# First gate and up units over two feature chunks and both columns, with 256-wide matmuls; 39 spins on a constant tile; gelu table behind column 1's copy

## Chip, cores, metric

One core of one Trainium2 chip. The metric is the device time of one execution in microseconds; lower is better. Before: 178.17 us (median of 6 runs, 177.86 to 178.23).

## The reference, cut to what matters

```
x  = A_x                                    # 1 x 2048 x 512, bf16
xn = layernorm(x)                           # over the last axis
h  = gelu(xn @ w_gate) * (xn @ w_up)        # 512 -> 1792
return x + irfft2(rfft2(xn) * W) + h @ w_down
```

The change touches the start only: normalising the first rows and the first gate and up matmuls.

## The kernel before

PE is the tensor engine, DVE the vector engine, ACT the scalar engine, POOL GpSimd, and SP issues the transfers. PSUM holds the tiles named `..._ps` in the kernel, into which its matmuls write. "Spins" are matmuls whose result is never used: they keep PE busy until the input is there, so that its granted clock rises from half to full speed ("released") early. (In the profile before, 128-wide matmuls start every 107 ns up to 6.49 us and every 55 ns from 6.78 on.) Four more of them, the "fillers" (`spin_on`), bridge the time between the first transposes and the first gate matmul.

The 2048 rows lie as 16 "columns" of 128 rows. Columns 0 and 1 go first: statistics on DVE, square root on ACT, normalisation on DVE, transposes on PE, copies from PSUM on ACT and DVE. Gate and up then run in units: `c0, n` are the first column and the number of columns, `f0, m` the first feature chunk of 128 and their number. The moving operand is `n` x 128 wide. The first four units (k < 4) split the contraction (four chunks `e`) in halves, so that the first half can start before all has landed.

```python
    spin = pc.tile([P, P], BF16, name="spin")
    ...
    nc.vector.memset(spin[:], 0.0)
    nc.vector.memset(eps_t[:], EPS)
    ...
    sp_ps = ps.tile([P, D], F32, name="sp_ps", tag="S", bufs=4)
    for k in range(37):
        pin(nc.tensor.matmul(sp_ps[:, :P], lhsT=spin[:], rhs=spin[:], start=True, stop=True))
    ...
        table = add("ACT", 1.3, lambda: A.activation(out=warm[:], in_=eps_t[:], func=AF.Gelu_apprx_tanh), [o["root", 1]], key=-1500, lat=1.3)
    ...
        o["copyt1"] = add("ACT", 0.4, lambda: f_Tc(1, 2, 2, A.copy), [o["t", 1], table], key=-1400)
    ...
        def mm_part(name, tag, W_, e0):
            if e0 == 0:
                b[name] = ps.tile([P, m, w], F32, name=name, tag=tag, bufs=2)
            for e in (e0, e0 + 1):
                for f in range(m):
                    T_.matmul(b[name][:, f], lhsT=W_[:, e, (f0 + f) * P:(f0 + f + 1) * P], rhs=rhs[:, e, :],
                              start=(e + f == 0), stop=(e == NE - 1), skip_group_check=True)
    ...
    todo = [(0, 1, 0, 4), (0, 1, 4, 4), (1, 1, 0, 4), (1, 1, 4, 4)]
    todo += [(2, 2, f, 2) for f in range(0, 8, 2)]
    todo += [(0, 4, f) for f in range(8, NFC)]
    todo += [(4 * sb, 4, f) for sb in range(1, NSB) for f in range(NFC)]
```

A planner in the program simulates the engines with assumed durations (`add(engine, duration, function, dependencies, key=...)`) and so fixes each engine's order when the program is built.

## Time and profile before

| | before |
|---|---|
| median time | 178.17 us |
| span of the profiled execution | 176.6 us |
| PE busy | 171.9 us (97%) |
| chain that ended last | PE 97% |
| first spin, first gate matmul, first up matmul | 1.05, 5.96, 10.13 us |
| end of the last matmul | 173.80 us |

Read it from the end: the last matmul's end plus some 2.8 us for the last addition and store is the span. PE runs without gaps from 5.96 on, so a date at which PE reaches a given piece carries over to the end unchanged, unless PE waits later.

### The profile page before, as it was taken

The numbers are of one execution on the slowest core, as the hardware profiler recorded it, in microseconds if no ns is written. First come the engines' busy times: TensorE is split into PE (matmuls) and PEld (weight loads), VectorE is DVE, ScalarE is ACT, GpSimd is POOL, SyncE is SP. The second block draws the span as 40 slices with busy tenths as digits, with TensorE's granted clock in tenths as the row PEclk, the third lists the DMA queues.
The fourth block names the chain that finished last, engine by engine and source line by source line (L and its number), as shares of the span: only waits on it lengthen the run. The fifth ranks groups of instructions, "written<-read, shape, count | busy, mean of one in ns | idle before, by whom it ended". The sixth has DMA issues, their size and how long they took to land.

```text
span 176.6 us, 3179 instructions
## 1 busy us (share of the span) xinstructions
PE 171.9 (97%) x1158; PEld 97.6 (55%) x1175; DVE 115.7 (66%) x253; ACT 96.8 (55%) x174; POOL 17.4 (10%) x38
## 2 busy tenths in 40 slices
PE   7999999999999999999999999999999999999993
PEld 7999844555545554555555445454444445444463
DVE  3459999987433699979899999643616325345333
ACT  4662299799646988898899955362112111211200
POOL 1020250504771000000000000000000000000000
PEclk9999999999999999999999999999999999999999
DMA  5999986432726902201211520200122222221212
GB/s 137 333 397 380 324 202 106 91 65 60 231 67 198 335 8 57 59 22 43 59 27 38 146 50 14 59 4 0 59 89 89 84 70 72 76 89 60 63 59 59
DMA packets 20847, 19.35 MB, mean 110 GB/s; under 512 B 8480, under 2 KB 17952, under 8 KB 20832
## 3 DMA queue, kind: packets, MB, share of 16 engines
q1 hardware_dynamic: 20416, 17.84, 34.3%
q0 software_dynamic: 416, 1.32, 2.5%
q8 instruction: 9, 0.15, 0.4%
q14 instruction: 6, 0.05, 0.1%
HBM read 13.38 MB, written 2.10 MB: 88 GB/s over the span
## 4 chain that ended last, share of the span: by engine, by line
PE 97%; issue 1%; DVE 0%
PE y_ps L837 27%; PE g_ps L492 25%; PE u_ps L492 25%; PE sp_ps L320 2%; PE g_ps L500 2%; PE yp L788 2%; PE bp L597 2%; PE u_ps L500 2%; PE gp L758 2%; PE dp L655 2%; PE y_ps L841 2%; PE ep L664 2%; PE tp L351 1%; PE sp_ps L324 0%; DVE y_sb L844 0%
## 5 line engine op out<-in xcount | busy, mean ns | idle before, releaser
L492 PE MATMUL u_ps<-xnT,Wu_sb 128*128 128x512 bf16 (+1 forms) x219 | 52.7, 363 | 0.2
L492 PE MATMUL g_ps<-xnT,Wg_sb 128*128 128x512 bf16 (+1 forms) x217 | 52.4, 363 | 0.4
L837 PE MATMUL y_ps<-Wd_sb,hT 128*128 128x512 bf16 (+2 forms) x247 | 50.5, 355 | 0.2
L510 DVE TENSOR_TENSOR hT<-u_ps,ge 128x512 bf16<-128x512 f32 x56 | 38.1, 688 | 17.7 <-PE u_ps L492 15.2
L505 ACT ACTIVATE ge<-g_ps 128x512 bf16<-128x512 f32 x56 | 33.4, 602 | 21.7 <-PE g_ps L492 19.0
L837 PEld LDWEIGHTS <-hT 128*128 128x128 bf16 x252 | 23.2, 98 | 22.5
L492 PEld LDWEIGHTS <-Wu_sb 128*128 128x128 bf16 x224 | 21.5, 98 | 20.8
L492 PEld LDWEIGHTS <-Wg_sb 128*128 128x128 bf16 x224 | 21.4, 98 | 20.2
L794 ACT CAST yf<-yp 128x512 bf16<-128x512 f32 x16 | 9.3, 586 | 40.5 <-PE yp L788 40.5
L844 DVE TENSOR_TENSOR y_sb<-y_ps,y_sb 128x512 bf16<-128x512 f32 (+2 forms) x18 | 11.1, 631 | 30.0 <-PE y_ps L841 30.0
L669 ACT CAST E<-ep 64x512 bf16<-64x512 f32 x32 | 18.5, 579 | 1.4 <-PE ep L664 1.0
L339 DVE BATCH_NORM_STATS2 stats<-x_t 128x6 f32<-128x512 bf16 x16 | 10.5, 674 | 3.2 <-DMA x_t<-in_A_x_dram 3.2
L454 ACT ACTIVATE xn<-x_t,nb,rstd 128x512 bf16<-128x512 bf16 x12 | 9.5, 814 | 1.0 <-POOL nb L370 1.0
L567 ACT CAST ds<-dp 128x512 bf16<-128x512 f32 x16 | 9.2, 598 | 0.8 <-PE dp L655 0.8
L567 ACT CAST Gs<-gp 128x512 bf16<-128x512 f32 x16 | 8.7, 592 | 0.6 <-PE gp L758 0.5
L567 ACT CAST Bs<-bp 128x512 bf16<-128x512 f32 x16 | 8.5, 611 | 0.5 <-PE u_ps L492 0.5
L800 DVE TENSOR_TENSOR lv<-yf 128x512 bf16<-128x512 bf16 x16 | 6.1, 421 | 1.5 <-ACT yf L794 0.6
L788 PEld LDWEIGHTS <-Gs 128*128 128x128 bf16 x64 | 4.8, 98 | 3.5
L807 DVE TENSOR_TENSOR yt<-lv 128x512 bf16<-128x512 bf16 x16 | 6.1, 422 | 0.3
L788 PE MATMUL yp<-CT,Gs 128*128 128x128 bf16 x64 | 6.0, 219 | 0.1
L841 PE MATMUL y_ps<-yt,RI_t 128*128 128x512 bf16 (+2 forms) x18 | 6.1, 355 | 0.0
L664 PE MATMUL ep<-ds,CT 128*128 128x512 bf16 x16 | 5.7, 379 | 0.0
(68 smaller groups left out, 134.1 us busy)
## 6 DMA issues: line engine op xcount, KB each, us to landing
F<-F SPq DMA_DIRECT2D x32, 64.0 KB, 2.0
y_sb<-in_A_x_dram SPq DMA_DIRECT2D x16, 128.0 KB, 2.1
out_dram<-y_sb SPq DMA_DIRECT2D x15, 128.0 KB, 1.7
x_t<-in_A_x_dram SPq DMA_DIRECT2D x7, 256.0 KB, 8.9
Wd_sb<-in_B_w_down_dram SPq DMA_DIRECT2D x1, 1792.0 KB, 8.5
Wg_sb<-in_B_w_gate_dram SPq DMA_DIRECT2D x2, 512.0 KB, 4.7
Wu_sb<-in_B_w_up_dram SPq DMA_DIRECT2D x2, 512.0 KB, 7.0
Wg_sb<-in_B_w_gate_dram SPq DMA_DIRECT2D x1, 768.0 KB, 10.4
```

What stands on the lines that cost most here:

```text
L339: V.bn_stats(out=st[:], in_=x_t[:, c, :])
L454: xn_op[c] = add("ACT", 0.72, lambda c=c: A.activation(out=xn[:, c, :], in_=x_t[:, c, :], func=AF.Identity, bias=nb[:, c:c + 1], scale=rst ...
L492: T_.matmul(b[name][:, f], lhsT=W_[:, e, (f0 + f) * P:(f0 + f + 1) * P], rhs=rhs[:, e, :], start=(e == 0), stop=(e == NE - 1))
L505: A.activation(out=b["ge"][:], in_=b["g_ps"][:], func=AF.Gelu_apprx_tanh)
L510: V.tensor_tensor(out=hT_of(sb, f0, m, o, w), in0=b["u_ps"][:], in1=b["ge"][:], op=ALU.mult)
L567: A.copy(out=o, in_=i)
L669: A.copy(out=b["E"][64 * h:64 * h + 64, r], in_=b["ep", h][64 * r:64 * r + 64])
L788: T_.matmul(t[:, q], lhsT=late["G"][:, q, c0 + j], rhs=IQ[q], start=(q == 0), stop=(q == 3), skip_group_check=True)
L794: A.copy(out=b["yf"][:, j], in_=b[j][:])
L837: T_.matmul(b[o][:], lhsT=hT_of(sb, f, 1, cl * P, P)[:, 0], rhs=Wd_sb[:, f, o:o + w], start=(f == 0), stop=False)
L841: T_.matmul(b[o][:], lhsT=late["RI"][:, c, :], rhs=late["yt"][:, c, o:o + w], start=False, stop=True)
L844: V.tensor_tensor(out=b["y"][:, o:o + w], in0=b[o][:], in1=b["y"][:, o:o + w], op=ALU.add)
```

## The change

Intent: make the first units cheaper by wider matmuls, start the spins earlier without waiting for DVE's fill, and take column 1's copy out from behind the load of the gelu table. The core of the diff (bookkeeping of dependencies cut):

```diff
-    spin = pc.tile([P, P], BF16, name="spin")
+    spin = nc.const_aps.tensor(1.0, (P, P), BF16)
...
-    nc.vector.memset(spin[:], 0.0)
...
-    for k in range(37):
-        pin(nc.tensor.matmul(sp_ps[:, :P], lhsT=spin[:], rhs=spin[:], start=True, stop=True))
+    for k in range(39):
+        pin(nc.tensor.matmul(sp_ps[:, :P], lhsT=spin, rhs=spin, start=True, stop=True))
...
-        table = add("ACT", 1.3, lambda: A.activation(out=warm[:], in_=eps_t[:], func=AF.Gelu_apprx_tanh), [o["root", 1]], key=-1500, lat=1.3)
...
-        o["copyt1"] = add("ACT", 0.4, lambda: f_Tc(1, 2, 2, A.copy), [o["t", 1], table], key=-1400)
+        o["copyt1"] = add("ACT", 0.4, lambda: f_Tc(1, 2, 2, A.copy), [o["t", 1]], key=-1400)
+        add("ACT", 1.3, lambda: A.activation(out=warm[:], in_=eps_t[:], func=AF.Gelu_apprx_tanh), [o["copyt1"]], key=-1300, lat=1.3)
...
-        def mm_part(name, tag, W_, e0):
+        def mm_part(name, tag, W_, e0, a, z):
...
-                    T_.matmul(b[name][:, f], lhsT=W_[:, e, ...], rhs=rhs[:, e, :],
+                    T_.matmul(b[name][:, f, a:z], lhsT=W_[:, e, ...], rhs=rhs[:, e, a:z],
...
+            args = "g_ps", gt, Wg_sb
+            g = part(*args, 1000, 5.7, 0, 0, P, ...)        # first half of e, column 0
+            g = part(*args, 1000.1, 5.7, 0, P, w, ...)      # first half of e, column 1
+            g = part(*args, 1000.2, 7.8, 2, 0, w, ...)      # second half, both columns, 256 wide
+            args = "u_ps", ut, Wu_sb
+            u = part(*args, 1001, 9.7, 0, 0, w, src)        # up: 256 wide throughout
...
+            u = part(*args, 1001.1, 11.0, 2, 0, w, [u])
...
-    todo = [(0, 1, 0, 4), (0, 1, 4, 4), (1, 1, 0, 4), (1, 1, 4, 4)]
+    todo = [(0, 2, f, 2) for f in range(0, 8, 2)]
```

## The prediction

The sum of the forecast came to -0.12 us, thus 178.04 us: 48 joins of two narrow matmuls at 2.4 ns each (115 ns, from the rates of the profile before), and 0 each for spins and table.

> **What bounds the kernel now.** I read the page's busy table and its chain first, then the chain in order of time, then the timeline of the first 14 us, and the DVE and ACT rows of the same stretch.
>
> ```profile
> span 176.6 us, 3179 instructions
> ...
> PE 171.9 (97%) x1158; PEld 97.6 (55%) x1175; DVE 115.7 (66%) x253; ACT 96.8 (55%) x174; POOL 17.4 (10%) x38
> ...
> PE 97%; issue 1%; DVE 0%
> ```
>
> PE carries the whole chain. A busy PE row alone doesn't prove that PE never waits[...]. So I checked it with the chain in order of time, where each piece has its start, its length and its matmul count:
>
> ```profile
> 1.05 4.12 PE sp_ps L320 x37
> 5.17 0.56 PE tp L351 x4
> 5.74 0.43 PE sp_ps L324 x4
> 6.17 0.78 PE g_ps L500 x8
> 6.94 0.22 PE tp L351 x4
> 7.17 3.13 PE g_ps L500 x56
> 10.29 1.79 PE u_ps L500 x32
> 12.08 0.45 PE tp L351 x8
> 12.53 1.79 PE u_ps L500 x32
> 14.31 1.75 PE g_ps L492 x16
> ```
>
> The reader can take three rates from it: 1.79/32 = 55.9 ns for a 128-wide matmul, 1.75/16 = 109.4 ns for a 256-wide one (the L492 rows of that stretch), and, from a later piece of 14 matmuls in 3.02 us, 215.7 ns for a 512-wide one. The program issues, after the first eight gate matmuls, 418 matmuls or transposes 128 wide, 79 of 256 and 625 of 512 (the program's own instruction list, as a few records are missing in the trace). That is 418 x 0.0559 + 79 x 0.1094 + 625 x 0.2157 = 166.8 us. Those eight end at 6.95, so a PE that never waits would end at 173.8; the chain's last PE piece ends at 173.82. **From 6.95 to the end PE loses less than 0.1 us to waits.** What is left is a store of some 2.8 us behind the last matmul, which the change doesn't touch.
>
> So the time is: the date at which real work starts, the cold rate at the start, and the number and width of matmuls. The start is a latency chain:
>
> ```profile
> 0.36 0.11 POOL L885 MEMSET const-bfloat16-1.0<- 128x1 bf16 x1
> ...
> 0.88 0.11 DVE L263 MEMSET spin<- 128x64 uint32 x1 [0.88 <-PEq L885]
> ...
> 1.05 4.13 PE L320 MATMUL sp_ps<-spin 128*128 128x128 bf16 x37 [1.05 <-DVE minus_half L266]
> ...
> 3.03 0.69 DVE L339 BATCH_NORM_STATS2 stats<-x_t 128x6 f32<-128x512 bf16 x1 [2.02 <-DMA x_t<-in_A_x_dram]
> ...
> 5.46 0.69 ACT L354 COPY xnT<-tp 128x256 bf16<-128x256 bf16 x2
> ...
> 6.17 1.28 ACT L412 ACT_TABLE_LOAD   x1
> ...
> 8.99 2.06 ACT L505 ACTIVATE ge<-g_ps 128x512 bf16<-128x512 f32 x4 [1.07 <-PE g_ps L500]
> ...
> 11.21 0.73 DVE L345 TENSOR_SCALAR xn<-x_t,mv,rstd 128x512 bf16<-128x512 bf16 x2 [1.18 <-POOL rstd L361]
> ```
>
> The input lands at 3.03, and statistics, normalisation, transposes and the ACT copy bring the first gate matmul to 5.96. The spins only fill the time before that, to warm PE's clock. They are not on this chain.
>
> [...] Here the spins start every (4.96 - 1.05)/36 = 109 ns, the gate matmuls from 5.96 to 6.49 still every 107 ns, and the transposes at 6.78 to 7.00 every 55 ns: the release came at about 6.6 to 6.7, although the page's PEclk row shows 9 from the start. [...]
>
> **The change, part by part.**
>
> *Wider matmuls.* Today the first four units are 4 feature chunks by 1 column, all 128 wide: 64 for gate and 64 for up. After, each has 2 chunks by 2 columns: the gate's first halves stay 128 wide (32), its second halves are 16 of 256, and up is 32 of 256. So 96 narrow ones become 48 wide ones: 48 x (2 x 55.9 - 109.4) = 48 x 2.4 = 115 ns[...]. All lie in the stretch where PE never waits: **-0.12 us**.
>
> *Spins.* The constant is filled in the preamble at 0.36 to 0.47, so PE no longer waits for DVE's fills; it can start where the other engines are released, at about 0.80 to 0.85, against 1.05. The 39 spins take 38 x 0.109 to the last start: 0.83 + 4.14 = 4.97, against 4.96 before. So the transposes at 5.03 are met as before: **0**, except through the clock release, below.
>
> *Gelu table behind column 1's copy.* Column 1's second copy runs today at 7.57, after the table load (6.17 to 7.46) and the dummy activation. After, it runs once its transposes end (7.00 + about 0.2), so at about 7.2 to 7.6. It is needed by the first second-half gate group, which PE reaches at 7.00 + 24 x 0.056 = 8.34; before, the column 1 units needed it somewhat later still. So column 1 is ready in time either way. The table then loads from about 7.6 to 8.9 and the dummy ends at about 9.1. The first gelu, today at 8.99, comes at about 9.1, the four of them end at 11.16 instead of 11.05. The fourth up unit needs the bank that the fourth gelu frees, at about 11.2; PE is there at about 10.03 + 3 x 0.4376 = 11.34. Slack is left: **0**.
>
> *Order.* The list of PE instructions is the same up to the first 512-wide units but for the widths. Afterwards the scheduler swaps some spectral groups with their gate or up neighbours; the sum of PE work is the same.
>
> Sum: -0.12 us, thus 178.16 - 0.12 = 178.04.
>
> **Rivals.**
>
> *The clock is released earlier.* If the release follows the start of the spins, it comes 0.2 us earlier, at about 6.45, and PE does the work of 0.2 us in half the time: -0.1 us. [...] For: the dates above. Against: it can't all be kept. Columns 2 and 3 are normalised by DVE from 11.21 to 11.94, a date set by a DMA at 8.53 and POOL. The fifth of the eight transposes follows 5 x 0.056 into a group whose weight loads start at 11.86, so at 12.08; it could start at about 11.99 (other transposes start 0.05 after their DVE row). So everything gained before 12 us is capped at about 0.09, of which the widths already take 0.08 by then; the second up halves add 0.04. **The cap leaves a total of about -0.13 to -0.2 whatever the clock does.** The banks freed by gelu cap it at a similar size.
>
> *A new wait replaces it.* Column 1's first gate group needs DVE's copy (7.09 to 7.38) and PE is there at 7.45; up needs its weights, which PE takes from 10.07 on today; the later swaps could put a spectral matmul ahead of the copy that feeds it. For: margins of 0.05 to 0.15. Against: before, the same copy met PE at the same date without a wait, and the planner left no wait in 167 us. It would make +0.1 to +0.3 us.
>
> *The spins on a broadcast constant run slower or the release comes later.* If they overran 5.03 they would delay the transposes one to one, +0.2 or more. Nothing in this profile speaks for it; I give it little.
>
> **Range and chances.** The sum is -0.12; the first rival pulls by a few hundredths, the second pushes by about as much with less chance. I say 178.0. Three runs of before lie between 177.98 and 178.18, and the profiled one took 178.28, so the noise is as large as the effect; the range is 177.75 to 178.3. 2% is 3.6 us, thirty times the effect; the only part of that size would be a lost clock, which nothing suggests: faster 0.01, same 0.985, slower 0.005.
>
> **What would show it.** In the profile after: spins from about 0.83, and the last transposes of column 0 still at about 5.35; the first gate matmul at 5.9 to 6.0; column 1's ACT copy ahead of the table load; the second gate halves and up at 109 ns each; up starting at about 10.0; the transposes of columns 2 and 3 at 11.75 to 11.85, waiting for DVE if the clock came early; the 256-wide gate group of columns 2 and 3 0.1 to 0.15 us before 14.15; and from there on the same pieces, shifted. The prediction is wrong if that shift is over 0.25, if DVE's second normalisation comes earlier, or if a wait on PE shows up later than 15 us.

## The result, and the profile after

After: 177.93 us (median of 6 runs, 177.78 to 178.14) against 178.17 us (177.86 to 178.23) for the kernel before in the same rounds. The ratio is 0.9991, with a 95% interval of 0.9978 to 1.0004. (A ratio is the mean time of one kernel's fast runs over that of the other's of the same rounds, so it is not quite the ratio of the medians.) By the 2% measure this is "same", and the interval includes no change at all.

The chain that ended last, in order of time, of the changed kernel (start, length, piece, count):

```profile
0.84 4.24 PE sp_ps L319 x39
...
5.63 0.22 PE sp_ps L323 x4
5.88 0.62 PE g_ps L499 x8
6.50 0.22 PE tp L350 x4
6.72 3.09 PE g_ps L499 x40
9.81 1.88 PE u_ps L499 x16
11.69 0.57 PE tp L350 x8
12.26 1.75 PE u_ps L499 x16
14.01 1.75 PE g_ps L491 x16
```

Set against the lines in the prediction: the gate piece of 56 took 3.13 us, its successor of 40 takes 3.09; the second half of up took 1.79, now 1.75. That is the width, as worked out. But the gate group of columns 2 and 3 starts at 14.01 instead of 14.31: 0.30 us earlier, not 0.12. The fillers show where it comes from: four took 0.43 us before (107 ns each) and take 0.22 now (55 ns each). In this execution the clock was already released. The timeline of the same kernel shows what PE then ran into (in brackets the idle time ahead, and what ended it):

```profile
5.87 0.45 PEld L499 LDWEIGHTS <-Wg_sb 128*128 128x128 bf16 x8 [0.20 <-DMA Wg_sb<-in_B_w_gate_dram]
...
6.56 3.25 PE L499 MATMUL g_ps<-xnT,Wg_sb 128*128 128x128 bf16 x40
...
6.76 0.37 ACT L353 COPY xnT<-tp 128x256 bf16<-128x256 bf16 x1 [0.72 <-PE tp L350]
7.15 1.28 ACT L423 ACT_TABLE_LOAD   x1
...
8.55 2.05 ACT L504 ACTIVATE ge<-g_ps 128x512 bf16<-128x512 f32 x4
...
9.77 1.64 PEld L499 LDWEIGHTS <-Wu_sb 128*128 128x128 bf16 x16 [0.24 <-DMA Wu_sb<-in_B_w_up_dram]
...
11.07 0.73 DVE L344 TENSOR_SCALAR xn<-x_t,mv,rstd 128x512 bf16<-128x512 bf16 x2 [1.18 <-POOL rstd L360]
```

Both weights now land after PE is ready for them, and the eight transposes take 0.57 us instead of 0.45, as the fifth waits 0.09 us for DVE's second normalisation. So the early clock release was about half given back to transfers. (An estimate from these dates: a release before 5.9 instead of at 6.73 saves half of 0.83 us, 0.42; of it 0.30 - 0.12 = 0.18 us was kept.) Two questions remained: is the early release a property of the change, and is the 0.12 us of the widths real?

The trace also keeps a record of each change of PE's granted clock. Before: the release is recorded at 6.73 us and the first close spacing of matmuls comes at 6.78, so the two agree. After: 4.86 us. (The page's PEclk row shows 9 from the first slice in both, since the time ahead of the first record is not counted as throttled.) All "release" dates below are such records.

### The profile page after: what moved, and what is told of

Same layout as the page of the kernel before. It is cut to its first block, busy times and chain, and to the rows that moved or that the text cites. A ratio compares the mean times of both kernels' runs of the same rounds, so it can differ in the third digit from the quotient of the medians.

```text
span 176.3 us, 3102 instructions
## 1 busy us (share of the span) xinstructions
PE 172.6 (98%) x1129; PEld 96.4 (55%) x1129; DVE 115.3 (65%) x252; ACT 97.1 (55%) x174; POOL 17.1 (10%) x38
## 4 chain that ended last, share of the span: by engine, by line
PE 98%; DVE 0%; issue 0%
PE y_ps L835 27%; PE g_ps L491 25%; PE u_ps L491 25%; PE sp_ps L319 2%; PE g_ps L499 2%; PE u_ps L499 2%; PE yp L786 2%; PE dp L653 2%; PE bp L595 2%; PE gp L756 2%; PE y_ps L839 2%; PE ep L662 2%; PE tp L350 1%; DVE y_sb L842 0%; PE sp_ps L323 0%
## 5 line engine op out<-in xcount | busy, mean ns | idle before, releaser
L491 PE MATMUL g_ps<-xnT,Wg_sb 128*128 128x512 bf16 (+1 forms) x224 | 53.1, 364 | 0.0
L835 PE MATMUL y_ps<-Wd_sb,hT 128*128 128x512 bf16 (+2 forms) x252 | 51.2, 355 | 0.0
L699 DVE TENSOR_TENSOR m<-X,TW 128x1024 bf16<-128x1024 bf16 x8 | 5.5, 688 | 0.2
```

The source lines that it names most:

```text
L835: T_.matmul(b[o][:], lhsT=hT_of(sb, f, 1, cl * P, P)[:, 0], rhs=Wd_sb[:, f, o:o + w], start=(f == 0), stop=False)
```

## The experiments

Twelve runs in four groups; each group shared its runs of the kernel before.

### Both kernels again, and the parts alone

`same_before` and `same_after` are the two kernels unchanged. `spins_only` is the kernel before with only the spins of the change; `wide_only` the one with only the units and widths; `table_only` (of the second group) with only the table's move:

```diff
# spins_only, on the kernel before
-    spin = pc.tile([P, P], BF16, name="spin")
+    spin = nc.const_aps.tensor(1.0, (P, P), BF16)
-    nc.vector.memset(spin[:], 0.0)
-    for k in range(37):
+    for k in range(39):
# wide_only, on the changed kernel: those lines and the table's two lines put back
# table_only, on the kernel before: only the table's two lines as in the change
```

Two theories stand in the expectations: S, that the clock's release follows from what the program issues, and F, that its date changes from execution to execution. Where F's reasons, and ranges of dates worked out from them, had not been shown by a trace, they are cut from the texts here and below.

> The kernel before, unchanged, once more: the null test, ratio 1.000 within 0.1%. Theory F [...]: [...] not again at 6.6 to 6.7[...]. Theory S (the release follows from what the program issues): release again at 6.6 to 6.7[...].

> The changed kernel, unchanged, once more: 177.9, ratio 0.9985 to 0.9995 against before. Theory F: [...] most likely later than the 4.85 of the first profile. Theory S: again at 4.8 to 4.9.

> Only the spins of the change (constant tile, 39). Theory S (the earlier start, or the constant, brings the release to 4.85): release at 4.8 to 4.9 and the time down by 0.15 to 0.25 us, to about 177.95. Theory F: the start is 0.2 us earlier, so the release is 0.2 us earlier on average and 0.1 us at most is gained; the time is 178.1, not to be told from before in 5 rounds.

> Only the units over two columns with 256-wide matmuls; old spins, old place of the table load. Both theories: 0.12 us less, 178.05; up's 16 matmuls before the transposes take 1.75 us instead of 32 in 1.79. The release is drawn as for before: S says 6.6 to 6.7, F says anywhere.

> The kernel before with only the gelu table moved behind column 1's copy. My step: no change of time, ratio 1.000; the copy starts at about 7.1 instead of 7.57, the first gelu at about 9.1. If column 1's copy had held the tensor engine, 0.1 us or more would be gained.

Measured: `same_before` 178.21 us, ratio 1.0003 (0.9986 to 1.0019); `same_after` 178.05, ratio 0.9999 (0.9983 to 1.0014); `spins_only` 178.16, ratio 1.0006 (0.9989 to 1.0024); `wide_only` 178.10, ratio 1.0000 (0.9984 to 1.0016); the kernel before in these rounds 178.05. `table_only` 178.18 against 178.22, ratio 1.0000 (0.9987 to 1.0012). No part, nor the whole, can be told from nothing by time; the 0.9991 of the first six runs was not repeated by the next five.

The dates of one profiled execution each tell more (us; the last column is the difference of the two before it, t3_later is told further down):

| kernel | first spin | clock released | columns 2, 3 normalised from | up starts | last matmul ends | up to end |
|---|---|---|---|---|---|---|
| before | 1.05 | 6.73 | 11.21 | 10.13 | 173.80 | 163.67 |
| same_before | 1.05 | 6.20 | 11.03 | 10.03 | 173.71 | 163.68 |
| table_only | 1.05 | 6.30 | 10.90 | 9.96 | 173.63 | 163.67 |
| spins_only | 0.84 | 4.94 | 11.00 | 9.81 | 173.49 | 163.68 |
| wide_only | 1.05 | 3.98 | 11.30 | 10.01 | 173.72 | 163.71 |
| after | 0.84 | 4.86 | 11.07 | 9.77 | 173.50 | 163.73 |
| same_after | 0.84 | 5.40 | 11.20 | 10.07 | 173.67 | 163.60 |
| t3_later | 0.84 | 3.96 | 10.79 | 9.66 | 173.26 | 163.60 |

Three readings follow.

*The widths are real and of the predicted size.* From up's start to the end, every kernel with narrow up matmuls takes 163.67 to 163.68 us, and the changed one, where no wait falls in, 163.60. The runs told further down agree: `before_x1_act`, with narrow up matmuls, has 163.67, and `one_spin`, `wg_on_act` and `after_x1_act`, with wide ones, have 163.59. Up's 32 joins (two narrow matmuls made one) at 2.4 ns are 0.077 us. Where the total is 163.71 and 163.73, the fifth transpose waited for DVE.

*The release is not tied to the program.* The program before had its release at 6.73 and 6.20 us, the changed one at 4.86 and 5.40, and `wide_only`, with the old spins on zeros, 3.98. Theory S named 6.6 to 6.7 and 4.8 to 4.9 and falls.

*What sets up's start changes from execution to execution.* In the very kernel that is unchanged the weights can be what PE waits for, as in `same_before` (timeline):

```profile
10.03 1.79 PEld L500 LDWEIGHTS <-Wu_sb 128*128 128x128 bf16 x32 [0.20 <-DMA Wu_sb<-in_B_w_up_dram]
```

and in `same_after` they landed 0.3 us later than in the first profile of the same kernel:

```profile
10.06 1.64 PEld L499 LDWEIGHTS <-Wu_sb 128*128 128x128 bf16 x16 [0.37 <-DMA Wu_sb<-in_B_w_up_dram]
```

For `table_only`, the step held: column 1's copy ran at 7.03 instead of 7.57, PE pieces of the same lengths, the same 163.67 behind up's start. The first gelu came at 8.83, earlier than the 9.1 expected; the clock was released 0.4 us earlier in this execution.

The expected ratio of `same_after`, 0.9985 to 0.9995, was not met (0.9999), but its interval doesn't exclude it.

### What the spins are worth: one_spin

```diff
-    for k in range(39):
+    for k in range(1):
     def spin_on():
-        for k in range(4):
+        for k in range(1):
```

> The changed kernel with 1 spin instead of 39 and 1 filler instead of 4; the tensor engine's steady work begins at 5.0 us. Theory F [...]: [...] the time up by half of the cold stretch after 5.9 us, 0.5 to 2.5 us, with a spread of the same size between runs. If the spins were idle filling only, the time would stay within 0.2 us of the changed kernel.

Measured: 179.49 us (178.74 to 179.84), ratio 1.0066 (1.0044 to 1.0088), so some 1.2 us over the kernel before of the same rounds. (The changed kernel did not run in them; the run cuts three of the four fillers as well.) The release came at 10.46 us. The timeline of `one_spin`:

```profile
5.79 1.01 PE L499 MATMUL g_ps<-xnT,Wg_sb 128*128 128x128 bf16 x8
...
7.02 4.91 PE L499 MATMUL g_ps<-xnT,Wg_sb 128*128 128x128 bf16 x40
11.77 1.91 PE L499 MATMUL u_ps<-xnT,Wu_sb 128*128 128x256 bf16 x16
```

The reader sees the piece of 40 take 4.91 us instead of 3.25 in the same view of the changed kernel, and up start 2.0 us later. As expected by F, and the spread of 1.1 us between runs is as large as the effect. Here the spins are no idle filling.

### The dates of many releases: bursts

```diff
+    gate = [pc.tile([P, P], BF16, name=f"gate{i}") for i in range(2)]
+    seen = pc.tile([P, 1], F32, name="seen")
+    for i in range(8):
+        for r in range(3):
+            pin(nc.vector.memset(Wd_sb[:], 0.0))
+        pin(nc.vector.memset(gate[i % 2][:], float(i % 2)))
+        for k in range(66 + i):
+            pin(nc.tensor.matmul(sp_ps[:, :P], lhsT=gate[i % 2][:], rhs=gate[i % 2][:], start=True, stop=True))
+        pin(nc.vector.tensor_copy(out=seen[:], in_=sp_ps[:, :1]))
     for k in range(39):
```

> The changed kernel behind eight bursts of 66 to 73 spins each, with an idle tensor engine of about 11 us ahead of each (three long fills on DVE), on a tile of zeros in bursts 1, 3, 5, 7 and of ones in 2, 4, 6, 8; results stay right and the total time, some 150 us longer, says nothing. Each burst draws its own date of release, 8 in one execution. Theory F: all changes of the clock lie on one grid of 3.413 us; [...] zeros and ones don't differ. Rival Z (zeros count less as activity, which would explain that the seven profiles with the constant were released 3.1 to 5.0 us after the first spin and three of four with zeros at 5.1 to 5.7): in the bursts of zeros the release comes over 1 us later than in those of ones at the same place in the grid.

Measured: the result was right; 317.9 us in one run of unknown state, which says nothing, as announced. All fifteen changes of the clock in the record lie on one grid, multiples of 3413 ns apart: releases at 18.22, 35.28, 52.35, 69.42, 86.48, 103.55, 124.03 and 141.10, throttles between them. From a burst's start to its release it took, in order, 4.72, 3.84, 3.40, 3.04, 2.86, 2.65, 5.96 and 4.16 us. The two that decide are the sixth (ones) and the seventh (zeros), in the timeline of `bursts`:

```profile
100.90 5.38 PE L325 MATMUL sp_ps<-gate 128*128 128x128 bf16 x71 [11.85 <-DVE gate L323]
118.07 7.02 PE L325 MATMUL sp_ps<-gate 128*128 128x128 bf16 x72 [11.79 <-DVE gate L323]
```

One more matmul, but 1.6 us more. The sixth burst starts 2.65 us ahead of a grid point and is released there (it fills 78% of the 3.41 us before it). The seventh starts 2.55 us ahead of one (75%) and isn't; it is released at the next. The fifth, on zeros, was released with 2.86 us (84%). So F's grid held for the fifteen changes of this run, and the dates of the eight bursts sort by where they met it: the four that had 2.65 to 3.40 us ahead of their first grid point were released there, the four that had 0.43 to 2.55 us at the next one. What decides it inside PE is not shown. The clock records of the other profiles agree (that of `before_x1_act` is empty), counted in stretches of 3.41 us back from a recorded change: none that was filled to 75% or less was followed by a release (in `before` 66%, with spins from 1.05 to 3.32), and every throttled one filled to 78% or more was (in `wide_only` 86%, from 1.05 to 3.98). Rival Z falls: bursts of zeros were released with 2.86 and 3.40 us of work, each at the first grid point after its start. (That the share differs between zeros and ones inside 75% to 84% isn't excluded.)

An estimate of what the earlier start is worth, from these dates: say that a start at `s` is released between s + 2.6 (between the 2.55 us that did not suffice and the 2.65 that did) and s + 6.0 (3.41 later; the longest burst took 5.96), with every date between equally likely. That gives 3.7 to 7.1 for the old start and 3.4 to 6.9 for the new; the dates in the table lie inside. A release after 5.9, where gate work begins, costs half of the excess (107 ns for a matmul in place of 55). Its mean is (7.06 - 5.9)^2 / (4 x 3.41) = 0.10 us for the old start, (6.85 - 5.9)^2 / (4 x 3.41) = 0.07 for the new: 0.03 us on average, before what the transfers take back. By this estimate it was luck that the first profile of before drew 6.73 and that of after 4.86.

### What width costs: narrow_all

All later gate and up matmuls are cut to 128 wide.

```diff
-                    T_.matmul(b[name][:, f], lhsT=W_[:, e, (f0 + f) * P:(f0 + f + 1) * P], rhs=rhs[:, e, :],
-                              start=(e == 0), stop=(e == NE - 1))
+                    for q in range(0, w, P):
+                        T_.matmul(b[name][:, f, q:q + P], lhsT=W_[:, e, (f0 + f) * P:(f0 + f + 1) * P],
+                                  rhs=rhs[:, e, q:q + P], start=(e + q == 0), stop=(e == NE - 1), skip_group_check=True)
```

> The changed kernel with all later gate and up matmuls cut into pieces 128 wide (64 of 256 into 128, 384 of 512 into 1536). Theory W (width only costs the fixed part of a matmul, 2.4 ns for a 256 and 7.9 ns for a 512, as the rates of the profile before give): 64 x 2.4 + 384 x 7.9 = 3.2 us more than the changed kernel, 181.1. [...]

Measured: 185.0 us (184.01 to 185.97), ratio 1.038 (1.0344 to 1.0417): some 7 us over the changed kernel, not 3.2. The expectation of the total missed. The chain of `narrow_all` in order of time says why:

```profile
17.64 0.89 PE g_ps L492 x16
...
48.13 0.31 issue
...
48.83 0.35 issue
...
49.40 0.50 issue
...
50.28 1.05 issue
...
53.12 1.71 PE g_ps L492 x16
```

Sixteen narrow matmuls take 0.89 us, 55.8 ns each, in place of 0.86 for four of 512: the rate, and with it some 3.1 of the 3.2 us, is confirmed. The rest is something else: around 48 to 51 us PE stands still with nothing to wait for ("issue", 2.2 us in the chain; by the starts of the matmuls 3.0 us are lost there), and the clock is then throttled for 3.41 us (recorded from 52.38 to 55.79), which costs half of it, 1.7 us. From up's start to the end this profile takes 171.30 us, 7.7 more than 163.60, and 3.1 + 3.0 + 1.7 = 7.8. The profiled run took 185.74 us. The recorded clocks of the four runs support this: 185.74 and 185.97 had a granted clock of 0.991, 184.01 and 184.27 of 1.000, so the throttled stretch is the 1.7 us between the two pairs. What causes the "issue" gaps stays open; the program has 5530 instructions in its profile instead of 3102, and no run separates that.

### Lifting the cap of the transfers: wg_on_act, before_x1_act, after_x1_act

Up's start is capped by landing dates (PE's load of up's first weights stood idle for them 0.24 us in the first profile after, 0.37 in `same_after`), so I tried to issue the early transfers sooner, using ACT's queue beside SP's.

```diff
# wg_on_act, on the changed kernel: first half of the first gate weights
+    pin(load_w(Wg_sb, 0, 1024, nc.scalar, e=slice(0, 2)))
     pin(nc.scalar.activation(out=warm[:], in_=eps_t[:], func=AF.Sqrt, bias=eps_t[:], scale=1.0))
     ...
-        for e in range(0, NE, 2):
+        for e in range(2 if T is Wg_sb else 0, NE, 2):
# before_x1_act and after_x1_act: second column of the input
+    pin(load_x(1, 1, nc.scalar))
     pin(nc.scalar.activation(out=warm[:], in_=eps_t[:], func=AF.Sqrt, bias=eps_t[:], scale=1.0))
     pin(load_x(0, 1))
-    pin(load_x(1, 1))
```

> The changed kernel with the first half of the first gate weights issued from the ACT queue at 0.8 us, ahead of ACT's table load, instead of as third transfer of the SP queue at 1.71. Theory D (what caps the gain are the landing dates of the transfers): everything behind it in the queue lands some 0.3 to 0.5 us earlier, up starts at about 9.55, columns 2 and 3 are normalised from about 10.7, no wait before the transposes, and the end comes 0.2 to 0.3 us earlier than in the changed kernel, about 177.7. Rival: ACT pays for the issue (table load and root later) or the second column of the input lands later behind the weights, the chain to the first gate matmul grows by the same, and nothing is gained or 0.3 us is lost.

> The kernel before with the second column of the input issued from the ACT queue at 0.8 us, ahead of ACT's table load, so that every later transfer of the SP queue is issued 0.43 us earlier. Theory D (landing dates cap the start): up's first weights land at about 9.4 instead of 9.77 to 10.1, but this kernel's tensor engine reaches them at 10.0 to 10.1 only when the clock comes late, so it gains 0 to 0.25 us, depending on the release. Rival: the second column lands behind the first weights as it did when those went first, and the time rises by 1 us.

> The changed kernel with the same move. Theory D: up's first weights at about 9.4, columns 2 and 3 normalised from about 10.7, up starts when the gate's second halves end, 9.55 with an early release, the transposes of columns 2 and 3 no longer wait, and the time is 0.2 to 0.3 us below the changed kernel: 177.7. If the gelu's banks cap it instead (first gelu 8.4 to 9.1), up still starts at about 9.8 and nothing is gained. Rival as for the other: 1 us lost.

Measured: `wg_on_act` 179.80 us (178.98 to 181.04), ratio 1.0097 (1.0059 to 1.0136), in two clusters, near 179.0 and from 180.6 to 181.0. `before_x1_act` 178.71, ratio 1.0057 (1.0024 to 1.009); `after_x1_act` 179.10, ratio 1.0071 (1.0046 to 1.0096). All three lose, by less than 2% but clear of noise; theory D's forecast of a gain was wrong. The rivals were right that time is lost, but not all on how. In `before_x1_act` and `after_x1_act` ACT paid nothing that mattered, and the second column did not land behind the weights, as the rival had it. The first column itself landed later: DVE starts on it at 3.89 and 4.06, against 2.96 to 3.43 in the eight profiles of the table:

```profile
3.89 0.69 DVE L339 BATCH_NORM_STATS2 stats<-x_t 128x6 f32<-128x512 bf16 x1 [2.88 <-DMA x_t<-in_A_x_dram]
```

In `wg_on_act` it was the second column, as its rival said, but the loss was 0.8 to 2.8 us and not 0.3. DVE takes this column's statistics ahead of the first column's normalisation, so the whole chain waited for it:

```profile
5.63 0.69 DVE L339 BATCH_NORM_STATS2 stats<-x_t 128x6 f32<-128x512 bf16 x1 [1.43 <-DMA x_t<-in_A_x_dram]
...
6.83 0.61 PE L351 MATMUL tp<-ident_t,xn 128*128 128x128 bf16 x4 [1.72 <-DVE xn L345]
...
8.25 4.89 PE L500 MATMUL g_ps<-xnT,Wg_sb 128*128 128x128 bf16 x40
```

The 1.72 us that PE then idled had a second price: the piece of 40 takes 4.89 us instead of 3.25. The clock record has a release at 4.94, a throttle at 8.35 and a release at 11.76. Here a released clock was lost again after 3.41 us with 1.72 us of idle time in them. How much idle time is enough doesn't come out of these runs: in `bursts` PE was idle for 1.8 us of the 3.41 us that ended at 21.63, and the clock stayed released. One throttled stretch costs half of 3.41 us, 1.7, and the two clusters lie 1.9 us apart in the mean: the three upper runs, the profiled one (181.04 us) among them, had a granted clock of 0.989 to 0.990 by the record, the three lower ones of 0.998 to 1.000.

That what is issued beside the first column takes bandwidth from it is the author's guess; no run separates this from other effects of the second queue. What the two runs with the second column on ACT's queue show is that nothing was gained, and that the first column landed 0.5 to 1.1 us later.

### Taking away the wait for column 3: t3_later

```diff
             if k == 3:
                 between["t", 2].deps.append(u)
-                between["t", 3].deps.append(u)
             u = part(*args, 1001.1, 11.0, 2, 0, w, [u])
+            if k == 0:
+                between["t", 3].deps.append(u)
```

> The changed kernel with column 3's transposes moved behind the first of up's four second halves. Where the normalisation of column 3 caps the gain (the wait of 0.09 us between the fourth and the fifth transpose), that wait is gone and the later groups start 0.1 us earlier for the same start of up: from up's start to the last matmul's end 163.60 instead of 163.73 us. Nothing that time alone could tell from the changed kernel: 177.9.

Measured: 178.10 us (177.70 to 178.36), ratio 0.9999 (0.9984 to 1.0014). In its profile, the chain in order of time:

```profile
9.79 1.78 PE u_ps L499 x16
11.58 0.22 PE tp L350 x4
11.80 0.44 PE u_ps L499 x4
12.24 0.22 PE tp L350 x4
12.46 1.31 PE u_ps L499 x12
13.77 1.75 PE g_ps L491 x16
```

No wait is left between the transposes, and up to end is 163.60, as expected. But this doesn't test the edit: DVE's second row ended at 11.53 here (10.79 + 0.74), and the fifth transpose in its old place would have come at about 11.64 (11.41 + 4 x 0.056), so it would not have waited either; and `same_after` has 163.60 without the edit. That execution is the shortest seen (span 176.0 us), but it also drew the earliest release of the table and the earliest landings of up's first weights and of columns 2 and 3; over six runs the version can't be told from the others. It beats neither kernel measurably.

## Why the prediction was right, step by step

*PE is the bound and never waits after the start.* Held: behind up's start the time was the same to 0.01 us in every profile of a kernel with narrow up matmuls.

*Widths, -0.12 us.* Held term by term: up's part 0.07 to 0.08 (163.67 against 163.60), the gate's 16 joins 0.04 (3.13 against 3.09), and `narrow_all` gave the same rate over 1600 narrow matmuls. The wholes, 178.17 to 177.93 and 178.05 to 178.05, are compatible with it but don't show it. The stated range of 177.75 to 178.3 holds the time of the kernel before too, so that the median fell into it says little.

*Spins, 0 except through the clock.* Held: the spins started at 0.84 and ended in time, and column 0's second transposes stayed at 5.34. (The prediction's date of 4.96 for the last spin is a misreading: 36 spacings of 0.106 us end at 4.86, and those of the changed kernel at 4.84; nothing hangs on it.) The clock's share is 0.03 us by the estimate above, where the first rival spoke of "-0.1 us". That rival supposed a release that follows the start; in the eight profiles of the table it came anywhere from 2.93 to 5.68 us behind the first spin.

*Gelu table, 0.* Held, by `table_only`.

*The cap, "a total of about -0.13 to -0.2 whatever the clock does".* This step failed. The pair of profiles shows -0.30, and with it two of the prediction's own signs of being wrong came true: a shift over 0.25, and DVE's second normalisation earlier (from 11.07 instead of 11.21). I had taken the date of columns 2 and 3 as fixed by the transfer at 8.53, from one profile. In eight profiles DVE's row starts anywhere from 10.79 to 11.30. (The slack of 0.09 us was read rightly, but the sum has a slip: the fifth transpose's weights load four spacings of 0.056 after 11.86, not five, which gives the 12.08 that is written.) The wait itself was seen twice, 0.09 us ahead of the fifth transpose in the first profile after and in `wide_only`; but the date that sets it moves by more than the effect. And the stricter cap in most executions was the one I had only listed among new waits: the landing of up's first weights. In five of the eight profiles their load stood idle 0.14 to 0.37 us for it, in a rerun of the kernel before too, which cost the matmuls 0.03 to 0.25 us. The median landed in the range since the widths' term was right and the rest averages out.

## What to carry to other kernels

Where PE ran without gaps, a wider matmul saved only its fixed part, here some 2.4 ns for each one saved (2 x 55.9 against 109.4 ns), so count the matmuls before hoping for more. Before an early start on PE is credited to a change, look at the release of its clock in several executions: here it came at dates from 3.96 to 6.73 us, at 6.73 and 6.20 for one and the same program, and one profile of each kernel would have credited 0.3 us to a change of which 0.12 can be shown. A gain in a start that is bound by transfers can be given back at the next landing, as half of it was here, and issuing an early transfer from a second queue can delay the very one that the chain begins with, here by 0.5 to 1.1 us.
